# A fused attention and feed-forward kernel: blocks of 1024 tokens in place of 512, more features by seven products, banks given out in turn, and a new order of the work

## The chip, the cores and the metric

The kernel runs on one core of a Trainium2 chip. The metric is the time of one execution on the device, in microseconds (us). The engines in play are PE (TensorE, the matrix products), ACT (ScalarE), DVE (VectorE), POOL (GpSimd, which here issues most loads) and SP (SyncE, which issues stores and transposing loads). Each engine takes its instructions from a queue of its own, in the order in which the program lists them; a semaphore holds an instruction until what it needs from another engine is done. PE's results go to PSUM, eight banks of 512 f32 columns for each of 128 partitions; ACT and DVE read them there.

## The reference

```
qn = q / (norm(q, axis=tokens) + 1e-6);  kn likewise          # q, k, v: 4 x 6080 x 256
s  = kn^T @ qn / tau                                          # 256 x 256 per batch
a  = softmax(s)                                               # along the last axis
x  = (v @ a) as 24320 x 256
h  = x @ w_in                                                 # 256 x 2048
out = gelu_tanh(h) @ w_out                                    # 2048 x 256
```

## The kernel before, in words

**Folding.** The kernel never forms x. Per batch it computes the 256 x 256 matrix of scores (`gram_row`, squares for the norms, `scores`), and multiplies the unnormalised exponentials with w_in into `AW` (2 x 128 channels by 2048 features, bf16; `aw_part` on PE, `aw_copy` from PSUM). Then h is `AW` times the transposed v, so features lie on partitions and tokens run along the free axis. The 2048 features are 16 chunks of 128, in 8 pairs. The next batch's scores are computed beside this batch's feed-forward work.

**Blocks.** The tokens of each batch are cut into 12 blocks (`BLK` = 512; the last one has 448), 48 in all. For block n:

- `mm1` (steps g0 to g7) computes one feature pair the plain way, four matmuls of 512 columns into a pair of PSUM banks, and `gelu` (G0 to G7) is one ACT instruction that reads them.
- `small` and `set_step` (steps w0.., w1.., w2..) compute two pairs at a time by a scheme with seven products in place of eight. It splits the block into two halves of tokens, the 256 channels into two halves, and the features into the two pairs of a *set* (`SETS`). Each of the products m1 to m7 is two matmuls of 256 columns here. `sums_v` and `sums_w` form the sums of v and of AW that they take. The products are gathered in one single bank, `rb`, and one pair of banks, `qp`: m1 starts `rb`; m5 starts the second half of `qp`; ACT copies `rb` into the first half of `qp` (step cq, line 613), after which m2 adds to it; m6 adds to `rb`; ACT saves m5 (y5, line 616); DVE adds `rb` and the saved m5 into `qp` (ap, line 618), after which m3 adds to it; m7 adds to `rb`; DVE forms another sum (ax, line 621); m4 adds to `rb`. Three gelus (Gq, Gr, Gx: lines 623, 628, 631) end it.
- So m6, which overwrites what cq reads, waits for cq; m7 waits for ap; m4 waits for ax. In the built program cq itself waits for whichever of m1 and m5 comes later. Each of these is a round trip from PE to ACT or DVE and back.
- The number of sets is 2 of 4 possible in most blocks, and 3 in the last batch (`sets_of`): 103 in all.
- `product` (M1A to M7B, line 726) multiplies the gelu's result with w_out by the same scheme of seven products; each half (A, B) is four matmuls of 256 columns. DVE forms the sums of the gelu's quarters (T1a, T2a to T4b, lines 687 to 703), and ACT and DVE combine the results (cq, y5, ap, ax, c11a) and turn them (`turn`) for the stores.

**Banks.** Four single banks and two pairs of banks. Each use has a fixed bank: `a` for the next batch's scores, `s` for `rb`, `r` and `p` for the second products, pairs `h` and `b` for `mm1` and `qp`.

**Order.** The order of all steps is written out in the lists `ORDER`, one string per block (`WINDOW` says which); the loop at the end reads a name at a time and issues that step's instructions. A suffix such as -1 or +3 takes the step from another block. Nothing reorders them: this list is the order of every engine's queue.

**Loads.** v is cast to bf16 through DRAM by POOL's queue (`cast_v`, lv) and transposed on load by SP's queue (`load_vt`, lt). q and k come in chunks of 6 rows (`load_one`). Both gate on the last matmul issued before them.

Of the kernel before, what the change touches and what calls it, by code (L numbers as in the profile page):

```python
# [18 lines left out]
def kernel(  # L19
# [23 lines left out]
    BLK = 512  # L43
    NB = (N + BLK - 1) // BLK
    PAIRS = FC // 2
    PE_BLOCKS = 2

    const = ctx.enter_context(tc.tile_pool(name="const", bufs=1))
    qkp = ctx.enter_context(tc.tile_pool(name="qkp", bufs=5))
    sqp = ctx.enter_context(tc.tile_pool(name="sqp", bufs=2))  # L50
    a1p = ctx.enter_context(tc.tile_pool(name="a1p", bufs=1))
# [3 lines left out]
    vts = ctx.enter_context(tc.tile_pool(name="vts", bufs=4))  # L55
    gp = ctx.enter_context(tc.tile_pool(name="gp", bufs=2))
    t1p = ctx.enter_context(tc.tile_pool(name="t1p", bufs=1))
    tsp = ctx.enter_context(tc.tile_pool(name="tsp", bufs=1))
    t4p = ctx.enter_context(tc.tile_pool(name="t4p", bufs=2))
    swp = ctx.enter_context(tc.tile_pool(name="swp", bufs=2))  # L60
    tvp = ctx.enter_context(tc.tile_pool(name="tvp", bufs=2))
# [5 lines left out]

# [4 lines left out]
    def chunks_of(b):  # L75
        sizes = [8, 7, 8, 8, 8, 8] if b == 0 else [6, 6, 6, 6, 6, 6, 6, 5]
        assert sum(sizes) == R
        res, r0 = [], 0
        for n in sizes:
            res.append((r0, n))  # L80
            r0 += n
        return res

    def with_rest(b, c):
        return REM > 0 and c == (1 if b == 0 else len(chunks_of(b)) - 1)

    qk_tiles = {}

    def after(inst, gate):

        if gate is not None:
            tc.add_manual_dep(inst.ins, gate.ins.name, mybir.DependencyInfo(
                mybir.DependencyClass.Sync, mybir.DependencyReason.DATA), reason="pace")

    def load_one(b, c, which, gate=None):
        r0, n = chunks_of(b)[c]
        t = qkp.tile([128, 8, 256], BF16, tag="qk"[which])
        src = (q, k)[which]
        after(nc.gpsimd.dma_start(
            out=t[:, 0:n, :],  # L100
            in_=src[b, 0 : R * 128, :].rearrange("(p r) c -> p r c", r=R)[:, r0 : r0 + n, :]), gate)
        if with_rest(b, c):
            after(nc.gpsimd.dma_start(out=t[:REM, n, :], in_=src[b, R * 128 : N, :]), gate)
        qk_tiles.setdefault((b, c), []).append(t)

    def load_first():


        r0, n = chunks_of(0)[0]
        assert not with_rest(0, 0)  # L110
        st = gp.tile([128, 2, n, 256], FP32, tag="g", name="qk_f32")
        for h in range(2):
            for which, eng in ((0, nc.sync), (1, nc.scalar)):
                eng.dma_start(out=st[:, which, h * 4 : h * 4 + 4], in_=(q, k)[which][0, 0 : R * 128, :].rearrange(
                    "(p r) c -> p r c", r=R)[:, r0 + h * 4 : r0 + h * 4 + 4, :])
        return st

    def cast_first(st):
        for which in range(2):
            t = qkp.tile([128, 8, 256], BF16, tag="qk"[which], name=f"first{which}")  # L120
            for h in range(2):
                if which == 0:
                    nc.scalar.activation(t[:, h * 4 : h * 4 + 4], st[:, 0, h * 4 : h * 4 + 4], AF.Copy)
                else:
                    nc.vector.tensor_copy(t[:, h * 4 : h * 4 + 4], st[:, 1, h * 4 : h * 4 + 4])
            qk_tiles.setdefault((0, 0), []).append(t)

    def load_qk(b, c):
        load_one(b, c, 0)
        load_one(b, c, 1)  # L130


# [3 lines left out]
    def load_last():  # L136
        c = len(chunks_of(0)) - 1
        r0, n = chunks_of(0)[c]
        assert n == 8 and not with_rest(0, c)
        qk_tiles[0, c] = [qkp.tile([128, 8, 256], BF16, tag="qk"[w], name=f"last{w}") for w in range(2)]  # L140
        for w, a, e in PIECES:
            nc.gpsimd.dma_start(
                out=qk_tiles[0, c][w][:, a:e, :],
                in_=(q, k)[w][0, 0 : R * 128, :].rearrange("(p r) c -> p r c", r=R)[:, r0 + a : r0 + e, :])

    v_bf = {}

    def cast_v(n, gate=None):
        b, blk = divmod(n, NB)
        t0 = blk * BLK  # L150
        cols = min(BLK, N - t0)
        vb = dram.tile([BLK, C], BF16, tag="vb", name=f"vb{n}")
        after(nc.gpsimd.dma_start(out=vb[:cols, :], in_=v[b, t0 : t0 + cols, :]), gate)
        v_bf[n] = vb

    vt_tiles = {}

    def load_vt(n):
        b, blk = divmod(n, NB)
        t0 = blk * BLK  # L160
        cols = min(BLK, N - t0)
        vT = vts.tile([128, 2, BLK], BF16, tag="vT")
        nc.sync.dma_start_transpose(out=vT[:, :, :cols], in_=v_bf.pop(n)[:cols, :])
        vt_tiles[n] = vT


    G, SS, ACC, SQ, SQR = {}, {}, {}, {}, {}

    def rows_of(b, c):
        r0, n = chunks_of(b)[c]  # L170
        rows = [(r, 128) for r in range(n)]
        if with_rest(b, c):
            rows.append((n, REM))
        return rows

    def new_squares(b, c):
        sq = sqp.tile([128, 8, 512], BF16, tag="sq", name=f"sq{b}_{c}")
        if with_rest(b, c):
            nc.vector.memset(sq[REM:, chunks_of(b)[c][1], :], 0.0)
        SQ[b, c] = sq  # L180

    def square(b, c, which, eng):
        if (b, c) not in SQ:
            new_squares(b, c)
        t = qk_tiles[b, c][which]
        n = chunks_of(b)[c][1]
        parts = [(128, slice(0, n))]
        if with_rest(b, c):
            parts.append((REM, slice(n, n + 1)))
        for np_, r in parts:  # L190
            o = SQ[b, c][:np_, r, which * 256 : which * 256 + 256]
            if eng == "act":
                nc.scalar.activation(o, t[:np_, r, :], AF.Square)  # L193
            else:
                nc.vector.tensor_mul(o, t[:np_, r, :], t[:np_, r, :])

    def square_rows(c, which, a, e, eng):
        if (0, c) not in SQ:
            new_squares(0, c)
        t = qk_tiles[0, c][which][:, a:e, :]  # L200
        o = SQ[0, c][:, a:e, which * 256 : which * 256 + 256]
# [5 lines left out]
    def fold_rows(b, c):  # L207

        n = len(rows_of(b, c))
        if n == 8:  # L210
            a1 = yout.tile([128, 4, 512], BF16, tag="ot", name=f"a1_{c}")
            nc.vector.tensor_add(a1, SQ[b, c][:, 0:4, :], SQ[b, c][:, 4:8, :])
            SQ[b, c] = a1
            n = 4
        SQR[b, c] = n

    FOLD = {}

    def fold(b, c):

        assert len(rows_of(b, c)) == 6
        sq = SQ.pop((b, c))
        a1 = a1p.tile([128, 3, 512], BF16, tag="a1", name=f"a1_{b}_{c}")
        nc.vector.tensor_add(a1, sq[:, 0:3, :], sq[:, 3:6, :])
        FOLD[b, c] = a1

    def fold_more(b, c, k):

        a1 = FOLD[b, c]
        if k == 2:  # L230
            nc.vector.tensor_add(a1[:, 0, :], a1[:, 0, :], a1[:, 1, :])
        elif k == 4:
            nc.vector.tensor_add(ACC[b], ACC[b], a1[:, 0, :])
        elif b in ACC:
            nc.vector.tensor_add(a1[:, 0, :], a1[:, 0, :], a1[:, 2, :])
        else:
            ACC[b] = accp.tile([128, 512], FP32, tag="acc", name=f"acc{b}")
            nc.vector.tensor_add(ACC[b], a1[:, 0, :], a1[:, 2, :])

    def gram_row(b, c, i):  # L240
        first = b not in G
        if first:
            G[b] = pM.tile([128, 2, 256], FP32, tag="a", name=f"G{b}")
        qt, kt = qk_tiles[b, c]
        rows = rows_of(b, c)
        r, np_ = rows[i]
        for jc in range(2):
            nc.tensor.matmul(  # L248
                G[b][:, jc, :],
                lhsT=qt[:np_, r, jc * 128 : jc * 128 + 128],  # L250
                rhs=kt[:np_, r, :],
# [3 lines left out]
    def ss_rows(c, which, rows=None):  # L255


        last = c == len(chunks_of(0)) - 1
        n = SQR.get((0, c), 8)
        rows = range(n) if rows is None else rows  # L260
        if c == 0:
            SS[which] = pM.tile([128, 2] if which == 0 else [128, 256], FP32,
                                tag="sp"[which], name=f"ss0{which}")
        sq = SQ[0, c]
# [13 lines left out]
    def ss_cols(b):  # L278

        SS[b] = pM.tile([128, 4], FP32, tag="a", name=f"ss{b}")  # L280
        for j in range(4):
            nc.tensor.matmul(SS[b][:, j : j + 1], lhsT=ACC[b][:, j * 128 : j * 128 + 128],  # L282
                             rhs=ones_f[:, 0:1], start=True, stop=True)

    def g_copy(b):
        S = smx.tile([128, 2, 256], FP32, tag="S", name=f"S{b}")
        nc.scalar.activation(S, G[b], AF.Copy)
        G[b] = S

# [185 lines left out]

# [475 lines left out]

# [270 lines left out]
```

## Time and profile before

| | us |
|---|---|
| median of 3 runs | 696.51 (696.39 to 696.59) |
| the profiled execution, its own time | 696.62 |
| its span, first to last instruction | 694.8 |
| PE / DVE / ACT / POOL busy in the span | 672.9 / 630.7 / 615.9 / 73.3 |
| matmul records in the span | 5426 |
| granted TensorE clock, mean | 0.997 |

An engine's busy time counts the stretches in which at least one of its instructions runs; consecutive instructions of an engine overlap a little at their ends, so the time from one start to the next is shorter than an instruction's own duration. A matmul's duration is a good deal longer than the time to the next one, since matmuls are pipelined. A row of the groups reads: line, engine, operation, output and input tile, shape, count, busy us, mean ns of one, idle time of the engine before them and what ended it.

### The profile page before, as it was taken

How to read it: one execution, taken by the hardware profiler on the slowest of the kernel's cores; microseconds unless marked ns; L12 is line 12 of the kernel's file. 1: busy time of each engine (PE TensorE's matmuls, PEld its weight loads, DVE VectorE, ACT ScalarE, POOL GpSimd, SP SyncE). 2: the span in 40 equal slices, each digit the busy share in tenths (PEclk: the TensorE clock that was granted, in tenths of full speed). 3: DMA queues.
4: the chain of work that ended last, by engine and by line, in shares of the span. 5: the costliest groups of instructions: out<-in, count | busy, mean ns of one | idle time of the engine just before them, and what ended most of it. 6: DMA issues, size and time to landing. Idle time of an engine off the chain costs nothing.

```text
span 694.8 us, 14338 instructions
## 1 busy us (share of the span) xinstructions
PE 672.9 (97%) x5426; PEld 531.3 (76%) x5501; DVE 630.7 (91%) x1245; ACT 615.9 (89%) x894; POOL 73.3 (11%) x135
## 2 busy tenths in 40 slices
PE   4999999999999999999999999999999999999996
PEld 2857787777778777777777777777777888888785
DVE  4489998999998989999999889999999999999996
ACT  5389989999889999998988999999888999999993
POOL 4321101101001001101010110010000000000000
PEclk9999999999999999999999999999999999999998
DMA  9997987896478777747687777583563463453325
GB/s 241 208 271 95 162 146 119 118 150 105 69 141 129 124 125 113 113 80 122 92 137 121 118 124 124 97 140 54 81 99 69 77 103 61 82 102 59 54 39 89
DMA packets 161462, 79.07 MB, mean 114 GB/s; under 512 B 148448, under 2 KB 152160, under 8 KB 160672
## 3 DMA queue, kind: packets, MB, share of 16 engines
q0 software_dynamic: 14448, 39.72, 34.7%
q1 hardware_dynamic: 145696, 37.14, 32.0%
q10 hardware_dynamic: 1248, 1.28, 0.6%
q8 instruction: 43, 0.70, 0.4%
q14 instruction: 27, 0.22, 0.1%
HBM read 78.91 MB, written 36.57 MB: 166 GB/s over the span
## 4 chain that ended last, share of the span: by engine, by line
PE 94%; DMA 4%; issue 1%; ACT 0%; DVE 0%; POOL 0%; DVEq 0%; ACTq 0%; POOLq 0%
PE r L726 24%; PE h L521 21%; PE p L726 18%; PE rb L597 13%; PE qp L597 10%; PE G L248 5%; DMA t<-in_k_dram 2%; PE awp L461 2%; DMA t<-in_q_dram 1%; PE ss L282 0%; PE ss L275 0%; PE vt_ps L325 0%; PE rk L406 0%; PE warm L370 0%; DVE vT_pe L331 0%
## 5 line engine op out<-in xcount | busy, mean ns | idle before, releaser
L726 PEld LDWEIGHTS <-wcomb 128*128 128x128 bf16 x2688 | 262.2, 98 | 43.2 <-issue 0.2
L531 ACT ACTIVATE g<-h 128x1024 bf16<-128x1024 f32 (+1 forms) x178 | 179.9, 1014 | 16.4 <-PE h L521 13.9
L726 PE MATMUL r<-t,wcomb 128*128 128x256 bf16 (+1 forms) x1152 | 163.5, 271 | 0.1
L521 PE MATMUL h<-vT,aw 128*128 128x512 bf16 (+1 forms) x560 | 153.7, 376 | 3.5
L623 ACT ACTIVATE g<-qp 128x1024 bf16<-128x1024 f32 (+1 forms) x103 | 104.7, 1016 | 7.3 <-PE qp L597 5.8
L726 PE MATMUL p<-g,wcomb 128*128 128x256 bf16 (+1 forms) x760 | 108.0, 272 | 0.0
L521 PEld LDWEIGHTS <-aw 128*128 128x128 bf16 x712 | 69.3, 98 | 49.3 <-DVE aw L364 0.6
L597 PEld LDWEIGHTS <-sw 128*128 128x128 bf16 x824 | 80.3, 98 | 25.5 <-issue 1.3
L193 ACT ACTIVATE sq<-t 128x1536 bf16<-128x1536 bf16 (+4 forms) x59 | 79.2, 1358 | 8.2 <-DMA t<-in_q_dram 8.2
L618 DVE TENSOR_TENSOR qp<-rb,yw 128x512 f32<-128x512 f32 (+1 forms) x103 | 70.8, 687 | 12.3 <-PE rb L597 9.5
L597 PE MATMUL rb<-tv,sw 128*128 128x256 bf16 (+1 forms) x412 | 77.9, 271 | 0.3 <-DVE qp L618 0.2
L621 DVE TENSOR_TENSOR xw<-rb,yw 128x512 f32<-128x512 f32 (+1 forms) x103 | 69.4, 674 | 3.9 <-PE rb L597 2.5
L613 ACT ACTIVATE qp<-rb 128x512 f32<-128x512 f32 (+1 forms) x103 | 59.7, 580 | 11.9 <-PE rb L597 6.8
L597 PEld LDWEIGHTS <-aw 128*128 128x128 bf16 x618 | 60.3, 98 | 12.7 <-issue 0.7
L631 ACT ACTIVATE g<-xw 128x512 bf16<-128x512 f32 (+1 forms) x103 | 63.4, 626 | 1.3 <-DVE xw L621 1.2
L616 ACT ACTIVATE yw<-qp 128x512 f32<-128x512 f32 (+1 forms) x103 | 61.2, 594 | 3.7 <-PE qp L597 1.9
L699 DVE TENSOR_TENSOR t<-g,t 128x1024 bf16<-128x1024 bf16 (+1 forms) x96 | 63.4, 667 | 0.6
L701 DVE TENSOR_TENSOR t<-g 128x1024 bf16<-128x1024 bf16 (+1 forms) x96 | 63.7, 672 | 0.0
L703 DVE TENSOR_TENSOR t<-t,g 128x1024 bf16<-128x1024 bf16 (+1 forms) x96 | 63.5, 668 | 0.0
L628 ACT ACTIVATE g<-rb 128x512 bf16<-128x512 f32 (+1 forms) x103 | 61.2, 596 | 2.2 <-PE rb L597 1.7
L248 PE MATMUL G<-t 128*128 128x256 bf16 (+1 forms) x352 | 59.6, 278 | 0.9 <-DMA t<-in_k_dram 0.9
L687 DVE TENSOR_TENSOR t<-g 128x2048 bf16<-128x2048 bf16 (+1 forms) x48 | 57.5, 1197 | 0.0
(137 smaller groups left out, 887.6 us busy)
## 6 DMA issues: line engine op xcount, KB each, us to landing
out_dram<-ot SPq DMA_DIRECT2D x174, 128.0 KB, 3.3
vb<-in_v_dram POOLq DMA_DIRECT2D x41, 256.0 KB, 4.3
t<-in_q_dram POOLq DMA_DIRECT2D x21, 384.0 KB, 4.8
t<-in_k_dram POOLq DMA_DIRECT2D x21, 384.0 KB, 6.3
wst<-in_moe_w_out_dram POOLq DMA_DIRECT2D x2, 1024.0 KB, 11.3
t<-in_q_dram POOLq DMA_DIRECT2D x3, 512.0 KB, 15.0
t<-in_k_dram POOLq DMA_DIRECT2D x3, 512.0 KB, 17.0
out_dram<-ot SPq DMA_DIRECT2D x12, 112.0 KB, 2.7
```

The source lines that it names most:

```text
L193: nc.scalar.activation(o, t[:np_, r, :], AF.Square)
L248: nc.tensor.matmul(G[b][:, jc, :], lhsT=qt[:np_, r, jc * 128 : jc * 128 + 128], rhs=kt[:np_, r, :], start=first and jc == 0, stop=jc == 1, ...
L521: mm = nc.tensor.matmul(hp[:, u, :cols], lhsT=AW[b][:, cc, fc * 128 : fc * 128 + 128], rhs=vt_tiles[n][:, cc, :cols], start=cc == 0, stop= ...
L531: nc.scalar.activation(gs(n)[:, 2 * p : 2 * p + 2, :cols], HP.pop((n, p))[:, :, :cols], AF.Gelu_apprx_tanh)
L597: GATE[0] = nc.tensor.matmul(acc[:, u * hc : u * hc + hc], lhsT=lhs[:, u * 128 : u * 128 + 128], rhs=rhs, start=m in (1, 5) and u == 0, st ...
L618: nc.vector.tensor_add(qp(n, i)[:, 1, :c], RB[n, i][:, :c], YW[n, i][:, :c])
L621: nc.vector.tensor_add(XW[n, i][:, :c], RB[n, i][:, :c], YW.pop((n, i))[:, :c])
L623: nc.scalar.activation(gs(n)[:, 2 * pa : 2 * pa + 2, :c].rearrange("p u (t x) -> p t u x", t=2), QP.pop((n, i))[:, :, :c].rearrange("p t ( ...
L631: nc.scalar.activation(gs(n)[:, 2 * pb : 2 * pb + 2, hc:c], two(XW.pop((n, i))[:, :c]), AF.Gelu_apprx_tanh)
L701: nc.vector.tensor_sub(o, quarter(n, 1, 1, f0, f1), quarter(n, 0, 1, f0, f1))
L703: nc.vector.tensor_sub(o, ts[2][:, f0:f1, :hc], quarter(n, 1, 0, f0, f1))
L726: nc.tensor.matmul(ACCS[n, acc][:, :hc], lhsT=wcomb[:, w, fc, :], rhs=x, start=first and k == 0, stop=k == 3, skip_group_check=True)
```

## The change

- Blocks have 1024 tokens (five per batch and one of 960; in the last batch the last 960 are cut into 512 and 448): 25 blocks in place of 48.
- A set is now one pair of features (two chunks of 128) on two halves of up to 512 tokens, so each of m1 to m7 is one matmul of 512 columns where it was two of 256. ACT's and DVE's steps of a set keep their shapes (512 or 1024 columns). Block 0 has 3 pairs in sets, blocks 1 to 18 have 5, blocks 19 to 22 have 7, block 23 has 4, block 24 none: 125 sets.
- `mm1` computes what is left, a pair and a half of the block at a time. `product` runs on halves of 512 tokens: 512 columns a matmul. The T sums and the combining steps have twice the columns each and half the count. T1 is formed in place in the gelu's tile, and T2 is formed from it.
- All banks are given out in turn: `take` hands out the bank that has been free longest, `give` returns it. The second products use up to two single banks at a time (u and p, then u and c).
- q and k chunks have 4 rows; `aw_copy` is all on DVE (`AW_ACT` is empty); pools are resized.
- `ORDER` is one list over all blocks and batches. Names are block:step, b1:step for the scores of batch 1; s4m6 is product m6 of the set of pair 4.

```diff
-    BLK = 512
+    HALF = 512
+    SIZES = [[1024] * 5 + [960]] * (B - 1) + [[1024] * 5 + [512, 448]]
...
-    vts = ctx.enter_context(tc.tile_pool(name="vts", bufs=4))
-    gp = ctx.enter_context(tc.tile_pool(name="gp", bufs=2))
-    t1p = ctx.enter_context(tc.tile_pool(name="t1p", bufs=1))
-    tsp = ctx.enter_context(tc.tile_pool(name="tsp", bufs=1))
-    t4p = ctx.enter_context(tc.tile_pool(name="t4p", bufs=2))
+    vts = ctx.enter_context(tc.tile_pool(name="vts", bufs=3))
+    gp = ctx.enter_context(tc.tile_pool(name="gp", bufs=3))
+    tp = ctx.enter_context(tc.tile_pool(name="tp", bufs=3))
...
+    FREE = {1: ["a", "s", "r", "p"], 2: ["h", "b"]}
+    def take(key, kind, shape, name, dtype=FP32):
+        tag = FREE[kind].pop(0)
+        t = (pM if kind == 1 else pH).tile(shape, dtype, tag=tag, name=name)
+        HELD[key] = (kind, tag)
+        return t, tag
+    def give(key):
+        kind, tag = HELD.pop(key)
+        FREE[kind].append(tag)
...
     def small(...):
-        for u in range(2):
-            GATE[0] = nc.tensor.matmul(acc[:, u * hc : u * hc + hc], lhsT=lhs[:, u * 128 : u * 128 + 128],
-                             rhs=rhs, start=m in (1, 5) and u == 0, stop=u == 1,
-                             skip_group_check=True)
+        GATE[0] = nc.tensor.matmul(acc[:, :hc], lhsT=lhs, rhs=rhs, start=i in (1, 5), stop=True,
+                                   skip_group_check=True)
...
+        if i == 1:
+            nc.vector.tensor_sub(quarter(m, 0, 1, f0, f1), quarter(m, 0, 1, f0, f1), quarter(m, 0, 0, f0, f1))
...
-    BANK = {1: "r", 6: "r", 7: "r", 4: "r", 5: "p", 3: "p", 2: "p"}
+    BANK = {1: "u", 6: "u", 7: "u", 4: "u", 5: "p", 3: "p", 2: "c"}
...
-        if b and p in (1, 4, 5, 6):
+        if b and p in AW_ACT:
...
-    w0ax w0m2 row2 row1 vs+1 M5A-1 w0Gq w0m4 M1A-1 T3b-1 w0Gr w1m5 row4 T3a-1 M1B-1 w1y5 T2b-1
+AW_ACT = ()
+10:G20 b2:f11.4 9:M6B 10:s3ax 9:ap 10:s3m3 10:s3m4 10:s4m5 10:s4cq 10:s3Gr 9:T4b 10:s4m6 10:s4m2
+10:s3m2 b2:ss 10:s4y5 10:s3Gx b2:sv 9:M3A 9:M3B 10:s4ap b2:pow 14:lv0 8:c11 10:s4m7 10:s5m1 10:s3Gq
```

## The prediction

> **What bounds the kernel now.** First the page's shares and its chain, then who PE waited for, then the durations of one instruction, then one place in order of time.
>
> ```profile
> PE 672.9 (97%) x5426; PEld 531.3 (76%) x5501; DVE 630.7 (91%) x1245; ACT 615.9 (89%) x894; POOL 73.3 (11%) x135
> PE 94%; DMA 4%; issue 1%; ACT 0%; DVE 0%; POOL 0%; DVEq 0%; ACTq 0%; POOLq 0%
> ```
>
> PE is busy 97% and is 94% of the chain that ended last. The view of waits, for PE alone (who waited for whom: us in total, times, longest):
>
> ```profile
> PE G L248 <- ACT first L123: 6.7, 1, 6.7
> PE G L248 <- DVE first L125: 2.6, 1, 2.6
> PE ss L269 <- DVE a L212: 1.1, 1, 1.1
> PE G L248 <- DMA t<-in_k_dram: 0.9, 1, 0.9
> PE h L521 <- DVE aw L364: 0.4, 1, 0.4
> PE rb L597 <- DVE qp L618: 0.2, 1, 0.2
> ```
>
> All but the last line lie in the first 38 us. After them PE waits 0.2 us in 650. Every round trip through ACT and DVE is covered by other matmuls, though DVE and ACT are about 90% busy. So there are two questions: how much matmul time goes, and whether the new order still covers the round trips.
>
> Durations of one (groups by shape; second number after the bar is ns):
>
> ```profile
> L521 PE MATMUL h<-vT,aw 128*128 128x512 bf16 x504 | 140.8, 379 | 3.4
> L618 DVE TENSOR_TENSOR qp<-rb,yw 128x512 f32<-128x512 f32 x94 | 65.2, 693 | 12.0 <-PE rb L597 9.3 <-ACT g L631 0.6 <-ACT yw L616 0.5
> L616 ACT ACTIVATE yw<-qp 128x512 f32<-128x512 f32 x94 | 56.3, 599 | 3.3 <-PE qp L597 1.6
> L613 ACT ACTIVATE qp<-rb 128x512 f32<-128x512 f32 x94 | 55.0, 585 | 11.2 <-PE rb L597 6.4 <-PE qp L597 1.2
> ```
>
> And the chain in order of time (start us, us) gives the spacing of matmuls when nothing waits:
>
> ```profile
> 48.16 1.74 PE h L521 x8
> 61.42 0.87 PE p L726 x8
> ```
>
> 1.74 / 8 = 0.217 us per 512 columns (0.216 from start to start in the records), 0.87 / 8 = 0.109 per 256. Last, the one late place, as the timeline has it:
>
> ```profile
> 647.89 0.38 PE L597 MATMUL rb<-tv,sw 128*128 128x256 bf16 x2
> 648.11 0.60 PE L726 MATMUL p<-t,wcomb 128*128 128x256 bf16 x4
> 648.38 0.70 DVE L618 TENSOR_TENSOR qp<-rb,yw 128x512 f32<-128x512 f32 x1 [0.28 <-PE rb L597]
> 648.54 0.38 PE L597 MATMUL qp<-tv,sw 128*128 128x256 bf16 x2
> 649.13 0.38 PE L597 MATMUL rb<-tv,sw 128*128 128x256 bf16 x2 [0.20 <-DVE qp L618]
> ```
>
> m6 (647.89) releases ap (648.38), ap releases m7 (649.13). From the second matmul of m6 at 648.00 to m7 are 1.13 us, and only six matmuls (0.65 us) stand between: too few, so PE idles. That is what a short cover looks like, and the price of one.
>
> **The change, part by part.** The sum is made against the profiled execution's 696.62 us, 0.11 above the median.
>
> *Matmul time.* From the issue order, before: 4242 matmuls of 256 columns x 0.109 = 462.4, 716 of 512 x 0.216 = 154.7, 350 of 224 and 56 of 448 (0.096 and 0.189 from start to start) 44.1, small ones 3: 664.2. After: 2370 of 512 x 0.216 = 511.9, 345 of 480 at 0.202 (between the rows) 69.7, 546 of 256 = 59.5, 32 of 448 and 56 of 224 11.4, small 3: 655.5. That is -8.7; column by column it is -9.2 (10,528 fewer columns at 1/2.4 ns, 2018 fewer matmuls at some 2.4 ns): I take **-9**. It is all on the path.
>
> *Round trips of a set.* cq: from the start of the matmul that releases it, 379 + 38 (median from PE's end to ACT's start in the records) + 585 + 50 (ACT's or DVE's end to PE's start) = 1.05 us to the matmul that waits; ap with 693 in place of 585: 1.17 us. Against it stands what PE has queued from the releasing matmul to the waiting one. Counted in both orders, with the rows above:
>
> - before: of 96 cq one is short (by 0.18 us), of 103 ap three (0.5 in all); the shortest cover is 0.76, the median 1.4.
> - after: of 114 cq **39 are short, by 0.54 us on average, 21.0 in all**; of 117 ap **39, by 0.46, 18.1 in all**; the shortest cover is 0.11, and 14 of the cq have 0.22 or less. ax is short once.
>
> An example is pair 4 of block 10: s4m5, then s4m6. cq waits for m5, m6 waits for cq, nothing stands between: 1.05 - 0.22 = 0.83 us in which PE does nothing, and M3A and all behind it wait with it. Where two short trips share PE time only one counts: 78 do not overlap, **36.4 us**.
>
> *Queues behind them.* The released step often stands behind others on its engine: a direct gelu takes 0.90 from start to start (the records), a T sum of 2048 columns 1.13 (1.2 long in its row). So I go back along ACT's or DVE's queue by up to eight instructions from each step that PE waits for, and compare the rows' sum from the matmul that releases the first of them with PE's between. Windows that share no PE time add to 64.5 us through one engine and **67.4 us** through both (106 windows). The same count gives 1.8 us for the order before, where the trace shows 0.6 (the last two lines of the waits). At 648 the rows give 1.05 for what took 1.13: 0.08 more, x 106 = **+8**.
>
> *ACT and DVE in sum.* From the same spacing, ACT's work grows by 15 us (18 more sets at 2.89 less the two gelus of 0.90 each that they replace; 12 `aw_copy` leave, 50 evacuations in place of 98), DVE's by 7 (18 sets at 1.21 and the copies, less 22 for T sums, adds and turns with half the count). To 631 and 638 of page time: neither bounds a span of 700. Their cost is in the windows above; above them I add nothing.
>
> *Loads and stores.* POOL issues 78 loads of q and k for the later batches where it issued 54, 0.55 us each: 13 us more on an engine busy 11%. SP issues 47 transposes for 45 and as many stores, in the old proportion, each behind the ones listed before it. Loads of q and k stand 7.8 us or more ahead of their use where landing takes 4.8 to 6.3. Two transposes (block 10, half 0; block 12, half 1) are listed 3.0 and 0.2 us ahead of a landing time of 4.9; unless SP reaches them sooner that is up to 7 us: range 0 to +7. Taken as 0, for SP is not held to PE's place in the list; if that cover goes, it is the 7.
>
> *PSUM in turn, larger tiles, T1 in place, start and end.* No instruction of their own. A wait for a bank or a buffer is a wait for its last reader, and is in the windows. The first 38 us keep the same loads and steps, and the end has the same last block of 448: 0, within 1 us either way.
>
> Sum: 696.6 - 9 + 67.4 + 8 = **763 us**. The windows are a floor, but for errors in their prices: round trips that pass more than twice between ACT and DVE are not in them.
>
> **A rule of the skill.** PE's clock. In this trace the first 16 matmuls of a Gram step (16.00 us) take 3.34 us, the same 16 later (20.80) 1.91, and the granted clock falls to 0.50 about 2.4 us after the last matmul; the one idle stretch that long inside (2.57 us) lies in the slow part at the start, so no row shows what it does to a warm PE. The Trainium skill, page "TensorE: Matmul & The Clock Gate", section "HAM oscillation — how this bites in real kernels", says that idle gaps over some 3.4 us throttle the array to half, and the next section that micro-idles between groups of matmuls can make it swing. By the first the sum stays, for no single trip here is that long; by the second it is rival 3.
>
> **The rivals.**
>
> 1. *The waits of single operations alone*: PE's own idling lets ACT and DVE run ahead, so nothing queues: 696.6 - 9 + 36.4 + 78 x 0.08 = **730**. For it: both have slack in sum. Against: a window's sum holds however far they ran ahead before it.
> 2. *Faster*: the trips are covered after all, because the copies don't wait as listed: 696.6 - 9 = **688**. It needs the m6 behind m5 to start within 0.2 us where the rows give 1.05; the turning point is 9 us exposed, 0.09 per window where I count 0.64. The place at 648, where a short cover did cost, speaks against it.
> 3. *The clock swings*: 25 blocks, each with one closing that costs what the slow Gram step shows, 1.43 us: +36, **799**.
> 4. *Late loads*: the two transposes and the casts ahead of them, with the stores on SP's queue: +7 to +20, **770 to 783**.
>
> **How the numbers follow.** The forecast 0.62, rival 1 0.13, rival 3 0.10, rival 4 0.10, rival 2 0.05. The range takes in rivals 1, 3 and 4: 728 to 805. A measurement of this kernel tells about 0.2%, 1.4 us; rival 2's 0.05 is faster but for 0.01, where the waits just eat the gain: faster 0.04, same 0.01, slower 0.95.
>
> **What would show it.** PE's busy share down to 86 to 90% at a clock near 1.0, with some 3470 records. In the view of waits, PE's `rb` and `qp` matmuls of `small` waiting for ACT's cq some 35 to 50 times, 18 to 30 us, and for DVE's ap as often, 15 to 25. ACT and DVE together over 5% of the chain. The 512-column matmul still 379 ns. Wrong, if PE's waits after the start sum to less than 30 us or the clock shows 0.5 within the span; and the cause is another, if waits on DMA lead.

## The result and the profile after

The changed kernel takes 762.52 us (762.11 to 762.78), the kernel before 696.55 beside it: a ratio of 1.0947, with a 95% interval of 1.0928 to 1.0966. The forecast was 763. The profiled execution took 762.63 us, with a span of 760.9 and a mean granted clock of 0.998.

Busy times and the chain that ended last, from the page of the changed kernel:

```profile
PE 687.2 (90%) x3422; PEld 333.9 (44%) x3483; DVE 637.5 (84%) x928; ACT 628.1 (83%) x930; POOL 87.8 (12%) x163
...
PE 59%; ACT 25%; DVE 6%; DMA 6%; issue 3%; POOL 0%; ACTq 0%; DVEq 0%; POOLq 0%
```

PE fell from 97% to 90% of a longer span, and ACT and DVE, which were nothing of the chain before, are 31% of it now, though each is *less* busy as a share than it was (83 and 84% after 89 and 91%). That is what exposed round trips look like: nobody is full, and everybody waits in turn.

The view of waits for PE, changed kernel (us in total, times, longest):

```profile
PE qp L610 <- ACT qp L622: 19.4, 28, 1.6
PE qp L610 <- DVE qp L627: 10.7, 20, 0.9
...
PE qp L610 <- ACT yw L625: 7.1, 12, 1.8
PE rb L610 <- DVE qp L627: 4.0, 7, 0.8
PE rb L610 <- ACT qp L622: 3.6, 8, 0.7
PE G L290 <- DMA k<-in_k_dram: 2.3, 1, 2.3
```

Before, the same view had 0.2 us after the start. L622 is cq, L625 y5, L627 ap. The tile named on PE's side is what to look at: most of the wait is by matmuls that write `qp`, not `rb`. The groups by shape (second number after the bar: mean ns of one) say which matmuls these are, and that on the mean no instruction got slower (one stretch of 3.4 us apart, at the end of this text):

```profile
L537 PE MATMUL h<-vT,aw 128*128 128x512 bf16 x436 | 113.3, 380 | 2.0 <-ACT g L550 0.4 <-DVE aw L393 0.4 <-ACT sq L262 0.4
...
L610 PE MATMUL qp<-tv,sw 128*128 128x512 bf16 x106 | 40.3, 381 | 20.4 <-ACT qp L622 17.5 <-ACT g L632 1.9 <-ACT g L550 0.5
...
L610 PE MATMUL qp<-vT,aw 128*128 128x512 bf16 x105 | 39.5, 380 | 10.6 <-ACT yw L625 6.5 <-DVE qp L627 3.9
```

and those of ap, cq and y5, from the same view for DVE and ACT:

```profile
L627 DVE TENSOR_TENSOR qp<-rb,yw 128x512 f32<-128x512 f32 x106 | 73.7, 696 | 45.0 <-PE qp L610 24.5 <-PE rb L610 10.0 <-ACT yw L625 8.9
...
L622 ACT ACTIVATE qp<-rb 128x512 f32<-128x512 f32 x106 | 62.8, 593 | 23.3 <-PE qp L610 18.8 <-PE rb L610 3.0
L625 ACT ACTIVATE yw<-qp 128x512 f32<-128x512 f32 x106 | 62.8, 600 | 9.5 <-PE qp L610 8.6
```

The `qp<-tv,sw` row is m5, the `qp<-vT,aw` row is m2. m5 takes sums of v and of AW and writes the *second* bank of `qp`; cq writes the *first*. m5 needs nothing of cq. m2 adds to the first bank; y5 reads and ap writes the second. Yet m5 waits 17.5 us for cq, and m2 waits 10.4 us for y5 and ap. One such place in the timeline (s2m1, s1m2, then s2m5 of block 21):

```profile
664.66 0.38 PE L610 MATMUL rb<-vT,aw 128*128 128x512 bf16 x1
...
664.91 0.38 PE L610 MATMUL qp<-vT,aw 128*128 128x512 bf16 x1
664.97 1.04 ACT L550 ACTIVATE g<-h 128x1024 bf16<-128x1024 f32 x1
666.05 0.58 ACT L622 ACTIVATE qp<-rb 128x512 f32<-128x512 f32 x1
666.68 0.38 PE L610 MATMUL qp<-tv,sw 128*128 128x512 bf16 x1 [1.40 <-ACT qp L622]
```

cq stands behind a direct gelu on ACT (664.97 to 666.01), starts at 666.05, ends at 666.63, and m5 starts 0.05 us later. The order lists cq ahead of m5, here just ahead. It does so in 39 of the 125 sets; the order before never does, in 103. So the question for the experiments was no longer whether round trips are exposed, but which: those that the data ask for, or those between two banks of one tile.

### The profile page after: what moved, and what is told of

It is laid out like the page before. It is cut to its first block, busy times and chain, and to the rows that moved or that the text cites. A ratio compares the mean times of both kernels' runs of the same rounds, so it can differ in the third digit from the quotient of the medians.

```text
span 760.9 us, 9845 instructions
## 1 busy us (share of the span) xinstructions
PE 687.2 (90%) x3422; PEld 333.9 (44%) x3483; DVE 637.5 (84%) x928; ACT 628.1 (83%) x930; POOL 87.8 (12%) x163
## 4 chain that ended last, share of the span: by engine, by line
PE 59%; ACT 25%; DVE 6%; DMA 6%; issue 3%; POOL 0%; ACTq 0%; DVEq 0%; POOLq 0%
PE u L715 15%; PE h L537 10%; PE rb L610 9%; PE qp L610 9%; PE p L715 7%; ACT qp L622 5%; PE c L715 5%; ACT g L632 4%; ACT g L550 4%; DMA qk<-in_k_dram 4%; ACT sq L262 3%; ACT yw L625 3%; PE G L290 3%; DVE qp L627 2%; ACT g L635 2%
## 5 line engine op out<-in xcount | busy, mean ns | idle before, releaser
L715 PEld LDWEIGHTS <-wcomb 128*128 128x128 bf16 x1400 | 136.4, 98 | 168.0 <-issue 28.0
L715 PE MATMUL u<-t,wcomb 128*128 128x512 bf16 (+3 forms) x581 | 143.2, 368 | 1.1 <-DVE p L764 0.2
L632 ACT ACTIVATE g<-qp 128x1024 bf16<-128x1024 f32 (+2 forms) x125 | 125.5, 1006 | 21.0 <-PE qp L610 18.5
L537 PE MATMUL h<-vT,aw 128*128 128x512 bf16 (+2 forms) x540 | 137.6, 377 | 2.1 <-ACT g L550 0.4
L627 DVE TENSOR_TENSOR qp<-rb,yw 128x512 f32<-128x512 f32 (+2 forms) x125 | 85.0, 683 | 50.2 <-PE qp L610 29.1
L630 DVE TENSOR_TENSOR xw<-rb,yw 128x512 f32<-128x512 f32 (+2 forms) x125 | 83.6, 670 | 22.5 <-PE rb L610 18.2
L622 ACT ACTIVATE qp<-rb 128x512 f32<-128x512 f32 (+2 forms) x125 | 72.5, 582 | 31.6 <-PE qp L610 22.1
L610 PE MATMUL rb<-tv,sw 128*128 128x512 bf16 (+2 forms) x244 | 89.2, 374 | 8.1 <-DVE qp L627 4.0
L715 PE MATMUL p<-g,wcomb 128*128 128x512 bf16 (+3 forms) x395 | 96.1, 368 | 0.4
L635 ACT ACTIVATE g<-rb 128x512 bf16<-128x512 f32 (+2 forms) x125 | 73.9, 592 | 11.7 <-PE rb L610 11.0
L625 ACT ACTIVATE yw<-qp 128x512 f32<-128x512 f32 (+2 forms) x125 | 72.7, 590 | 12.6 <-PE qp L610 11.4
L537 PEld LDWEIGHTS <-aw 128*128 128x128 bf16 x552 | 53.5, 98 | 64.2 <-issue 5.2
L638 ACT ACTIVATE g<-xw 128x512 bf16<-128x512 f32 (+2 forms) x125 | 77.5, 624 | 3.1 <-DVE xw L630 2.9
L696 DVE TENSOR_TENSOR t<-g,g 128x2048 bf16<-128x2048 bf16 (+3 forms) x50 | 58.1, 1162 | 0.1
L694 DVE TENSOR_TENSOR t<-g,g 128x2048 bf16<-128x2048 bf16 (+3 forms) x50 | 57.9, 1162 | 0.2
```

What stands on the lines that cost most here:

```text
L537: GATE[0] = nc.tensor.matmul(o.rearrange("p (t x) -> p t x", t=2) if t == 2 else o, lhsT=AW[b][:, cc, fc * 128 : fc * 128 + 128], rhs=x, s ...
L610: GATE[0] = nc.tensor.matmul(acc[:, :hc], lhsT=lhs, rhs=rhs, start=i in (1, 5), stop=True, skip_group_check=True)
L622: nc.scalar.activation(qp(m, p)[:, 0, :hc], RB[m, p][:, :hc], AF.Copy)
L625: nc.scalar.activation(YW[m, p][:, :hc], qp(m, p)[:, 1, :hc], AF.Copy)
L627: nc.vector.tensor_add(qp(m, p)[:, 1, :hc], RB[m, p][:, :hc], YW[m, p][:, :hc])
L630: nc.vector.tensor_add(XW[m, p][:, :hc], RB[m, p][:, :hc], YW.pop((m, p))[:, :hc])
```

## The experiments

What a run should take was worked out with a replay: the built program's queues, one per engine, with the semaphores that each instruction waits for, and the durations of the profile's rows. From the first product h to the last matmul it gives 649.6 us for the kernel before and 709.5 for the changed one, where the traces show 651.1 and 718.3.

**1. Banks apart, all three pairs.** The waits are drawn by the tile framework from the accesses to a tile. The edit names the pairs of instructions between which none is wanted, whichever of the two is listed first. The last four lines keep what is needed: m2 waits for cq, and an m5 listed behind its cq waits for the last gelu that read its pair of banks.

```diff
+    def apart(m, p, name, inst):
+        BY[m, p, name] = inst
+        for a, b in APART:
+            if name in (a, b):
+                other = BY.get((m, p, b if name == a else a))
+                if other is not None:
+                    tc.declare_no_dep(inst.ins, other.ins, reason="two banks")
+        if name == "m2":
+            after(inst, BY[m, p, "cq"])
+        if name == "m5" and (m, p, "cq") in BY:
+            after(inst, LASTG.get(QTAG[m, p]))
...
+APART = (('m5', 'cq'), ('m2', 'y5'), ('m2', 'ap'))
```

> The changed kernel with its order untouched, but the waits between the two halves of a qp tile taken away: m5 and cq, m2 and y5, m2 and ap touch different banks and need nothing of each other (m2 keeps its wait for cq, m5 its wait for the bank's last reader). Theory A (most of the exposed time is waits between the two banks, which the tile framework draws for a PSUM tile as a whole and the data do not ask for): a replay of the instruction streams with the rows' durations falls from 709.5 to 652.6 us from the first product to the last matmul, so 762.5 - 57 = 705 us (698 to 715), PE waits of some 12 to 18 us left. Rival B (the true round trips m1-cq-m6 and m6-ap-m7 with ACT's and DVE's queues behind them: other waits take the place of those removed): 745 to 760. Rival C (larger blocks and banks in turn leave ACT and DVE too little room): as B.

Measured: 706.74 us (706.16 to 707.75), ratio to before 1.0147 (1.0132 to 1.0162). 55.8 us of the loss are gone with the same order, blocks, banks and instructions. PE's waits that are left, after the start:

```profile
PE qp L625 <- ACT g L550: 3.6, 8, 0.9
PE qp L625 <- ACT g L649: 2.9, 7, 0.7
...
PE G L290 <- DMA k<-in_k_dram: 2.4, 1, 2.4
PE rb L625 <- DVE ot L755: 1.7, 1, 1.7
```

Waits of m5 for cq and of m2 for y5 are gone; what comes first now is m5 waiting for the gelu that last read its pair of banks, which a bank that is used again does ask for. The place shown above, 46 us earlier here:

```profile
618.69 0.38 PE L625 MATMUL rb<-vT,aw 128*128 128x512 bf16 x1
...
618.90 0.38 PE L625 MATMUL qp<-vT,aw 128*128 128x512 bf16 x1
619.78 0.58 ACT L639 ACTIVATE qp<-rb 128x512 f32<-128x512 f32 x1
...
619.80 0.39 PE L625 MATMUL qp<-tv,sw 128*128 128x512 bf16 x1 [0.52 <-ACT g L550]
```

m5 now runs beside cq (619.80 and 619.78), not behind it, and PE's idle time there is 0.52 us where it was 1.40.

**2 and 3. One pair of waits at a time.** `APART` holds ("m5", "cq") alone, or the two pairs of m2 alone.

> Only the wait between m5 and cq taken away (39 of 118 sets list cq ahead of m5). Theory A: the replay gives 709.5 to 679.2, so 762.5 - 30 = 732 us (726 to 738), and the waits of m2 for y5 and ap stay. Rivals B and C: 755 to 762, the wait turns up at m6.

> Only the waits of m2 for y5 and ap taken away. Theory A: the replay gives 709.5 to 685.6, so 762.5 - 24 = 738 us (732 to 745), and m5 goes on waiting for cq, some 25 to 30 us. Rivals B and C: 755 to 762.

(39 of 118 in the first of these expectations is a miscount of the sets: it is 39 of 125.)

Measured: 733.61 us (733.44 to 733.93) without the waits between m5 and cq, 737.89 (737.80 to 738.37) without those of m2: 28.9 and 24.6 us, together 53.5 of the 55.8 that both give. First lines of PE's waits, of the one and of the other (the waits of the start left out):

```profile
PE qp L625 <- DVE qp L644: 10.8, 19, 0.9
...
PE qp L625 <- ACT yw L642: 4.8, 10, 1.8
```

```profile
PE qp L625 <- ACT qp L639: 22.6, 30, 1.7
```

Each edit takes away its own rows. Without those of m2, the rows of `qp` and `rb` for cq stay (22.6 and 3.6 us after 19.4 and 3.6). Without those between m5 and cq, the rows for ap stay (10.8 and 4.0 after 10.7 and 4.0), and y5's falls from 7.1 to 4.8. With them goes m6's wait for cq (`rb`, 3.6 us in 8 times, to 0.2 in 1), for where m5 is listed first it was cq that waited for m5, and the edit lifts that, too. The two causes add; neither wait was covering for the other, against what rivals B and C say.

**4. The kernel before, banks apart.** The same declarations in `small` and `set_step` of the kernel before.

> The kernel before with the same waits taken away. Theory A: its order lists m5 ahead of cq in every set and covers the rest; the replay changes by 0.0: 696.5 within 1. Rivals B and C say the same; a fall of over 3 us would mean that the waits between banks were part of the time before, too.

Measured: 696.59 us beside 696.65, ratio 0.9999 (0.9990 to 1.0009). The kernel before has the same waits in its program, and its order covers them all. So these waits alone cost nothing, and the rest of the change without them (run 1) costs 10 us; the loss is mostly the two together.

**5 and 6. The loss made in the kernel before.** If that is so, it can be had without larger blocks or banks in turn, by listing m5 behind cq in the kernel before:

```diff
+        for n in range(NN):
+            for i in "01":
+                cq, m5, y5 = (f"w{i}cq", n), (f"w{i}m5", n), (f"w{i}y5", n)
+                if cq in STEPS and STEPS.index(m5) < STEPS.index(cq):
+                    early = STEPS.index(y5) < STEPS.index(cq)
+                    STEPS.remove(m5)
+                    STEPS.insert(STEPS.index(cq) + 1, m5)
+                    if early:
+                        STEPS.remove(y5)
+                        STEPS.insert(STEPS.index(m5) + 1, y5)
```

The loop takes the sets w0 and w1 alone: 91 of the 103 sets; the third set of a block, w2, keeps its order.

> The kernel before, blocks and banks untouched, with one step moved: in every set m5 is listed directly behind its cq (and y5 behind m5 where it stood ahead), where it stood ahead of m1. Theory A (a PSUM tile is waited for as a whole, so m5 now waits for a cq that works on the other bank): the replay goes from 649.6 to 690.0 us, so 696.5 + 40 = 737 us (728 to 745), PE waits for cq about 60 times. Rival B (what costs is the new blocks and their true round trips; in the blocks before there is room): below 705.

> The same order as in the run with m5 behind cq, with the waits between the two banks of a pair taken away. Theory A: 30 of the 40 us come back; the replay gives 660.1, so 707 us (701 to 712); what is left is the later y5 and what stands behind it on ACT. If the moved steps themselves cost the time, it stays near 737.

Measured: 740.99 us (740.85 to 741.16) and, with the banks apart, 709.55 (709.43 to 709.98). The first line of PE's waits in the first of them:

```profile
PE qp L597 <- ACT qp L613: 22.2, 57, 1.1
```

It is gone in the second, and 31.4 us with it. The moved steps by themselves cost 12.9 us. The blocks of 512 lose the same way as soon as the order lists the two steps the other way round.

**7. Banks last freed first.** One word, on top of run 1:

```diff
-        tag = FREE[kind].pop(0)
+        tag = FREE[kind].pop()
```

> The changed kernel with the waits between banks taken away, and PSUM banks given out last freed first, not in turn: the bank just read is then written next. The prediction put the handing out in turn at 0. If it is part of what the new order leans on, the replay says 652.6 to 706.7, so 706.7 + 54 = 761 us (745 to 775), with h waiting for gelus on ACT some 40 times. If it costs nothing either way: 706.7 within 3.

Measured: 761.40 us (761.22 to 764.13), 54.7 more than run 1. h waits for a gelu 35 times. PE's waits:

```profile
PE h L537 <- ACT g L550: 12.4, 19, 1.1
...
PE h L537 <- ACT g L649: 7.4, 12, 1.1
```

A product now gets the bank that ACT is still reading. The Trainium skill, page "Perfetto Trace Analysis", section "Optimizing Tensor Performance", says that independent groups of matmuls should rotate through different banks so that ACT's and DVE's reading of one overlaps the next; the 54.7 us agree. Handing out in turn is not what made the changed kernel slow: this order depends on it.

**8. The order alone.** All else as in the changed kernel, whole-tile waits included: the same 3557 steps, listed anew.

```diff
 ORDER = """
-0:g00 b0:aw2 b0:aw5 b1:lq0 ...
+(the same steps; found by moving single steps and keeping what shortens the replay)
```

> The changed kernel with nothing but the ORDER string written anew, the same 3557 steps, by a search over the replay in which a PSUM tile is waited for as a whole: blocks, sets, banks in turn and every instruction are kept. If the order is what costs (theory A, sharpened: blocks, banks and true round trips leave enough to cover with), the replay's 647.4 us stands against 649.6 for the kernel before (696.6) and 652.6 for the run with banks apart (706.7): 647.4 + 47 to 54 = 694 to 702 us, waits for cq, y5 and ap under 6 us. If blocks of 1024 with two pairs of banks leave too little work to cover with (rival): 725 or more.

Measured: 701.30 us (699.72 to 705.06), ratio 1.0070 (1.0051 to 1.0088). Busy times, and PE's largest wait after the start:

```profile
PE 674.9 (97%) x3483; PEld 334.3 (48%) x3483; DVE 634.1 (91%) x928; ACT 623.5 (89%) x930; POOL 88.5 (13%) x163
```

```profile
PE qp L610 <- ACT g L550: 1.7, 2, 1.1
```

The waits for cq and ap sum to 1.8 us in the view, and none for y5 is left. 61 us came back with nothing but the list. So blocks of 1024 with two pairs of banks leave enough work to cover every trip with, the needless ones too; the order that came with the change does not use it.

**9 to 12. Both at once, and orders with margins.** The banks apart and an order searched with that, and then three orders searched with 0.11 us more on every step of ACT and DVE and 3.5 us more on every load (run 10 is the order alone, 11 and 12 have the banks apart).

> An order written anew by the same search, with the waits between banks taken away as well. The replay gives 647.1 us: 694 to 701, and no more than 2 us away from the run with the order alone, since both orders leave 9 to 10 us of PE idle in the replay, most of it in the first 20 us of products. If it is over 5 us faster, the waits between banks still cost something in the re-laid order.

> The ORDER string alone written anew, by the same search with 0.11 us more on every ACT and DVE step and 3.5 us more on every load, so that short overruns and late loads are covered too. The replay at plain durations gives 649.0 us (the re-laid order before: 647.4, measured 701.3), 11.7 us of PE idle with 0.06 us added to each ACT and DVE step as the one before, but with loads 5 us later 29 in place of 63. If what was left over in that run (16 us between matmuls in 101 places) is late loads and overruns, this one gives 695 to 701; if it is the order's tightness as such, 701 to 706.

> The waits between banks taken away, and an order from the search with the added margins. The replay gives 646.0 us (before: 649.6, with banks apart and the order untouched 652.6): 646.0 + 47 to 54 = 693 to 700. If late loads (5.6 us behind a store in the first order of this kind) were what made 713 of it, they are gone here.

> As the run before, from another start of the search: the replay gives 647.3 us, and with loads 5 us later 21 us of idle where the other has 29: 694 to 701, with the smaller spread over executions if late loads make the spread.

Measured: 713.12 (708.68 to 717.19), 701.62 (701.19 to 702.66), **698.26** (698.17 to 699.70) and 710.96 us (708.90 to 713.11). Run 11 is the best version of the changed kernel, and it is still 1.0026 (1.0016 to 1.0036) of the kernel before: no version of it came out faster. Run 10 lies at the border of its two expectations and settles nothing about what was left of run 8. Runs 9 and 12 missed, and for a reason of their own, for the most part in one place each: PE idles 13.9 and 15.3 us after the start, where in run 11 it idles 7.1. Run 12, PE in the timeline:

```profile
419.60 0.38 PE L625 MATMUL rb<-tv,sw 128*128 128x512 bf16 x1
423.71 0.58 PE L290 MATMUL G<-k,q 128*128 128x256 bf16 x2 [3.73 <-DMA k<-in_k_dram]
427.24 0.61 PE L625 MATMUL rb<-vT,aw 128*128 128x512 bf16 x1 [2.96 <-DVE ot L755]
427.65 1.48 PE L290 MATMUL G<-k,q 128*128 128x256 bf16 x6
428.93 0.63 PE L625 MATMUL rb<-tv,sw 128*128 128x512 bf16 x1
...
430.38 0.38 PE L625 MATMUL qp<-vT,aw 128*128 128x512 bf16 x1
```

and the stretches around it (busy us and instructions of PE, PE's weight loads, DVE, ACT and POOL; the last three numbers are the granted clock, the DMA share and GB/s):

```profile
418.00:420.00 2.00, 1.98 (x13) 0.98 (x10) 0.93 (x2) 1.97 (x5) 0.00 (x0) 1.00 0.47 63
...
422.00:424.00 2.00, 0.29 (x2) 0.20 (x2) 0.00 (x0) 0.00 (x0) 0.00 (x0) 0.82 1.08 216
...
426.00:428.00 2.00, 0.76 (x3) 0.42 (x4) 1.53 (x3) 0.05 (x1) 0.00 (x0) 0.50 1.09 227
...
430.00:432.00 2.00, 2.00 (x11) 0.98 (x10) 1.77 (x4) 1.98 (x4) 0.69 (x2) 0.97 0.89 111
```

A load of k lands late, then a turned tile waits for an earlier store (DVE's 7.4 us for `out_dram<-ot`), while SP's queue, which issues the stores, stood 25.5 us between 380 and 430 us at transposing loads whose `vb` had not landed. Run 9 has a single wait of 4.74 us behind such a store. The replay priced loads and stores at one duration each, whatever else moves; as far as these two traces show, that is where it failed.

## Why the prediction was right, and what it did not see

*Matmul time, -9.* Held. The traces of runs 11 and 4 have a record for each matmul, and run 4 has the order and the time of the kernel before. From the start of the first product to that of the last matmul run 11 takes 653.1 us, and in 14.7 of them a matmul starts later than the usual spacing allows (by over 15 ns), which leaves 638.4. Run 4 takes 650.8, less 3.0: 647.8. That is -9.4. Spacing and duration of a 512-column matmul stayed at 216 and 379 to 381 ns.

*Round trips and queues, +67.4 + 8.* Held in size: 66.0 measured plus the 9 gained is 75. In the trace it is 53.8 us of idle PE in 102 waits of over 60 ns after the first 38 us (before: 0.3 in 2), and each wait costs some 0.16 us more than its idle time (below), 16 us; with the -9 that explains 60 of the 66. The other 6 are in the records, too. Some 70 matmuls start late without any idle time to show for it, by 6.5 us in all, where the kernel before has 26 by 2.2 us: waits too short to outlast the matmul before them. And some 1.4 us are matmuls at half clock (below). The trace lacks 61 matmul records, so these counts are rough. That the forecast of 763 came within 0.5 us is closer than such terms can promise, with the +8 not shown: in part it is luck.

*What the trips are.* Here the prediction was incomplete, and its example misleads. It counted every wait in the built program alike and described them as the cycle m1, cq, m6, ap, m7. Its example, m6 directly behind m5, is a place where cq waits for m5: a wait between banks that it took as given. The runs show that 55.8 of the 75 us were waits between two banks of one PSUM tile, which no data ask for, and the trace names m5 and m2 for them, where the prediction named `rb` and `qp` together. Its 39 short cq trips are as many as the sets that list cq ahead of m5, but that is chance. Counted again from the order, with the rows' spacings, 39 are short by 21.3 us: 22 run from m1 through cq to m5, 16 from m5 through cq to m6 or m2, and one alone from m1 to m6, which the data ask for. The other 17 sets that list cq ahead of m5 have cover enough. So the list already held the answer, had each trip been asked which bank it touches. Of the waits forecast, those for cq came as said: 36, 23.0 us (forecast 35 to 50, 18 to 30). Those for ap came short: 27, 14.7 us (forecast as often as cq, 15 to 25). The wait for y5, 7.1 us in 12 times, was in the sum but not in the list of what to look for.

*The +8 for hand-over* is right in sum only. The replay without it ends 8.8 us below the trace; but it ends 1.5 below it for the kernel before, too, and it has no half clock in it (1.4 us, below), so hand-over is not shown to be the cause.

*ACT +15, DVE +7.* Busy times rose by 12.2 and 6.8, and neither bounds: with the order laid anew they run at 89 and 91% and PE at 97%.

*PSUM in turn, 0.* Not wrong as put, since bank waits were in the windows; but run 7 shows that the order loses 54.7 us without it.

*Loads, 0 to +7.* One wait, 2.3 us, for a load of k at the start of the second batch's scores, and not for the two transposes that were named. The clock fell behind it (below).

*The clock as a sign of being wrong.* The prediction called itself wrong if the clock showed 0.5 within the span. It did, for 3.4 us of 760.9, behind that wait for k (below). The sign was too strict: the price was some 1.4 us, and the sum did not need it.

*The rivals.* Rival 1 (single operations alone, 730) fell with the time, which is 32 us above it; the place at 664 us shows a cq that stood behind a gelu, but the share of the queues was not tested apart. Rival 2 (688, the copies don't wait as listed) describes what run 1 makes true, and then the time is 706.7. Its turning point, 9 us exposed, fits: run 11 has 14.7 us of late starts where run 4 has 3.0, 11.7 more against 9.4 gained, and ends 1.6 us behind the kernel before. Rival 3 (the clock swings at each of 25 closings, 799) fell: one drop in the changed kernel, not 25. Rival 4's mechanism, stores on SP's queue, turned up only in runs 9 and 12.

## What to carry to other kernels

When an order, or a planner, treats two halves of a buffer as independent, look in the built program whether the waits are drawn per half or for the whole buffer: here a PSUM tile of two banks was waited for as one, and 56 of 75 us of lost time were waits that the data did not ask for. In the view of waits, read not only who waits for whom but for which tile, and ask whether the two touch the same bank. A change of blocks, banks and order together is judged in parts: with the order laid anew, the same blocks cost 0.7%, with the banks apart as well 0.3%, and not 9.5%.

## What the runs showed of the hardware

*A wait costs PE more than the idle time that the profile shows.* From the first product to the last matmul, the two runs on the kernel before with m5 behind cq differ by 31.8 us, and by 22.4 us of idle PE. The other 9.4 fall on 58 waits more (those of over 60 ns): 0.16 us each, which is what a matmul's duration exceeds the time to the next one (379 - 216, or 273 - 109 ns). After a wait that part is not overlapped, and the profile counts it as busy. The 102 waits of the changed kernel say the same: 53.8 us of idle PE, but 70.5 us by which the matmuls behind them start later than the usual spacing, 0.16 us more for each.

*The clock: the length of a wait alone does not decide.* In the changed kernel PE stood idle 102 times, up to 2.3 us, at a mean granted clock of 0.998. But behind the longest of these waits the clock fell to 0.50 for 3.4 us, from 54.3 to 57.7 us, and the matmuls took 0.63 us from 0.38 (the second view is of stretches, as above):

```profile
53.50 0.38 PE L290 MATMUL G<-k,q 128*128 128x256 bf16 x2 [2.32 <-DMA k<-in_k_dram]
...
55.26 0.63 PE L610 MATMUL qp<-tv,sw 128*128 128x512 bf16 x1
```

```profile
54.00:56.00 2.00, 2.00 (x8) 0.84 (x7) 0.55 (x1) 0.07 (x1) 0.00 (x0) 0.58 1.19 249
...
58.00:60.00 2.00, 1.19 (x7) 0.49 (x6) 1.76 (x4) 1.97 (x4) 0.54 (x1) 1.00 0.96 157
```

Waits of this length do not always do it. The same wait for k took the clock down for 3.4 us in runs 2 (2.33 us of idle PE) and 10 (2.14), but not in runs 1 and 3 (2.36 each) and 11 (1.95). In run 12 a wait of 2.35 us at 51 us did it, in run 7 one of 1.41 us at 552 us with another of 0.80 us just ahead of it; the changed kernel's other waits, of up to 1.8 us, left the clock at 1.00. In run 12 the idle stretch of 3.73 us, and in run 9 one of 4.74 us, took the clock to 0.50 for 6.8 us each. Those microseconds at half speed come on top of the wait. What decides at 1.4 to 2.4 us is not shown. The Trainium skill, page "TensorE: Matmul & The Clock Gate", section "HAM oscillation — how this bites in real kernels", puts the limit at idle gaps over some 3.4 us: the two long stretches agree, but five shorter ones, of 1.41 to 2.35 us, took the clock down as well, so here that limit is no safe one. Its section "A second HAM failure mode: psum-queue depth-cycling" lets micro-idles between groups of matmuls set the clock swinging; the 102 waits here brought one drop, behind the longest of them.
